# A gate vector computed by four column tiles of the matmul array instead of full-width matmuls, in a tuned attention and feed-forward kernel

## The chip, the cores and the metric

The kernel runs on one core of a Trainium2 chip. The metric is the device time of one execution in microseconds (us); each version is run several times, and what is quoted is the median. Every run used for a verdict is of the fast state. The trace of one execution, taken by the hardware profiler, gives a slightly shorter span than the timed runs: 739.1 us against a median of 741.06 us (740.49 to 744.32, three runs) for the kernel before.

Engines: PE is the matmul engine, PEld its weight loads, DVE the vector engine, ACT the scalar engine, POOL and SP the two that here mostly issue transfers. PSUM is the memory into which PE writes; this kernel uses it as eight banks of 128 partitions by 512 fp32.

## The reference

Two branches on the same input x (2048 rows of 1024, bf16) are mixed by a gate, which is one number per row:

```python
g = sigmoid((x * gate_w).sum(-1, keepdims=True))      # the gate, this case's subject
a = attention(x)        # 32 heads of 32; each row sees 8 rows, 2 apart, itself and backwards
b = (gelu(x @ w_gate) * (x @ w_up)) @ w_down          # 1024 -> 3584 -> 1024
return g * a + (1 - g) * b
```

## The kernel before

The rows are cut into four chunks of 512, and two chunks make a super-chunk: chunks 0 and 1, then 2 and 3. Per super-chunk the phases on PE are: qkv projections, gate logits, the FFN's first two products, then the down projections. Most products use Strassen's scheme with seven block products instead of eight. DVE must first form sums and differences of weight blocks (here called ring forms, because the weights live in a ring of buffers) and of x blocks (x forms, T1 to T4). DVE also does all of the attention's arithmetic except the exponentials.

No order is written by hand. Streams of operations are merged by a scheduler that gives every operation a modelled start, takes the smallest one, and so fixes each engine's order when the kernel is built. Each engine is handed its own list of instructions in that order.

```python
class Weave:                                   # cut
    def _start(self, op):
        ...
        t = self.clk[op.eng]
        for d in deps:
            t = max(t, d.end + (0.04 if d.eng == op.eng else self.LAT + op.lag))
        return t
    def run(self, streams):                    # of all streams' next ops the earliest is emitted
        ...
                if t is not None and (best is None or t + s[0] < best[0]):
                    best = (t + s[0], t, s, op)
...
w.run([(0.0, main()), (0.0, loads()), (0.1, wforms()), (0.1, x_forms()), (0.1, qkv_forms()),
       (0.15, preps()), (0.3, attention()), (0.5, scores())])
```

The gate of a chunk takes eight matmuls, one for each of the eight contraction tiles of 128. The gate weight column is broadcast over all 128 columns of the array, so all 128 output rows of the bank hold the same logits. A transpose in blocks of 32 then puts the logits of 512 rows onto partitions:

```python
def gate(c):
    i, free = bank_take()
    def go():
        for kt in range(KT):                                  # KT = 8
            nc.tensor.matmul(banks[i][:], lhsT=gcol[:, kt:kt + 1].to_broadcast([P, P]), rhs=xT(c, kt),
                             start=(kt == 0), stop=(kt == KT - 1))
    o = pe(KT, go, ...)                                       # modelled cost: 8 matmuls
    yield o
    zt = work.tile([P, SC], F32, tag="u2", bufs=2, name="zt") # buffers shared with u2q below
    e = dve(0.63, lambda: nc.vector.transpose(out=zt[:], in_=banks[i][:]), [o])
    yield e
    bank_give(i, e)
    zc = small.tile([P, SC // 32], F32, tag="zc", bufs=2, name="zc")
    yield dve(0.1, lambda: nc.vector.tensor_scalar(out=zc[:], in0=...zt..., scalar1=ZMAX, scalar2=-ZMAX,
                                                   op0=ALU.min, op1=ALU.max), key=("zc", c))
    ...
def gate_exp(c):                                              # ACT; needs its exp table
    e = act(0.1, lambda: nc.scalar.activation(out=ez[:], in_=zc[:], func=ACT.Exp), [("zc", c)], table="exp", ...)
```

The second super-chunk's gates stand right before its qkv products. The first of these use x as it is (`(0, 0)`, B11); the next need T1 and the first group of ring forms, the next T2 and the second group:

```python
yield from parts[2]                 # down projection of chunk c0
if more:
    yield from halo(c0 + 2)
    yield from gate(c0 + 2)
    yield from gate(c0 + 3)
    yield from qkv_pair(c0 + 2)
...
# qkv_pair, per product, cut:
o = prod(A[t], which, (0, 0), B11, t, True, [fr])             # no form needed
...
o = prod(Dk[t], which, 0, T1, t, True, [fr])                  # ring form 0, one per contraction tile, and T1
    ... ACT copies the bank to m5q
o = prod(Bk[t], which, 1, T2, t, False, [ev["seed", t]])      # ring form 1 and T2
    ... ACT copies the bank to u2q    (tag "u2", bufs=2)
```

Of the kernel before, what the change touches and what calls it, by code (L numbers as in the profile page):

```python
# [9 lines left out]
ALU = mybir.AluOpType  # L10
# [126 lines left out]
def kernel(  # L137
# [61 lines left out]
    banks = [psum.tile([P, SC], F32, name=f"ps{i}") for i in range(8)]  # L199
    xbuf = persist.tile([P, NB, NWIN * AC], BF16)  # L200
    gcol = consts.tile([P, KT], BF16)
    ident = consts.tile([P, P], BF16)
    w = Weave(nc, tc)
    n = NWIN * AC
    V = nc.vector.tensor_tensor
# [1 line left out]
    def xT(c, kt):  # L207
        return xr[:, 2 * (c % 2) + kt // KH, kt % KH, :]
# [18 lines left out]
    def bank_take():  # L227
        best = min(range(len(bank_free)), key=lambda i: -1.0 if bank_free[i][1] is None else bank_free[i][1].end)
        return bank_free.pop(best)

    def bank_give(i, op):
        bank_free.append((i, op))
# [41 lines left out]
        nc.tensor.matmul(banks[7][:], lhsT=warm[:, 0:P], rhs=warm, start=True, stop=True)  # L274
    wj = consts.tile([P, 1], F32)
    nc.scalar.activation(out=wj[:], in_=warm[:, 0:1], func=ACT.Exp)
    make_identity(nc, ident[:])
    nc.vector.memset(kT[0][:, :, 0:HALO], 0.0)
    nc.vector.memset(vT[0][:, :, 0:HALO], 0.0)
    with nc.allow_non_contiguous_dma(reason="gate vector, one element per partition"):  # L280
# [398 lines left out]

    def gate(c):  # L680
        i, free = bank_take()

        def go():
            for kt in range(KT):
                nc.tensor.matmul(banks[i][:], lhsT=gcol[:, kt:kt + 1].to_broadcast([P, P]), rhs=xT(c, kt),  # L685
                                 start=(kt == 0), stop=(kt == KT - 1))
        o = pe(KT, go, ([free] if free else []) + ([("x", c, kt) for kt in range(KT)] if c else []), key=("z", c))
        yield o
        zt = work.tile([P, SC], F32, tag="u2", bufs=2, name="zt")
        e = dve(0.63, lambda: nc.vector.transpose(out=zt[:], in_=banks[i][:]), [o])  # L690
        yield e
        bank_give(i, e)
        zc = small.tile([P, SC // 32], F32, tag="zc", bufs=2, name="zc")
        yield dve(0.1, lambda: nc.vector.tensor_scalar(out=zc[:], in0=zt[:].rearrange("p (b j) -> p b j", j=32)[:, :, 0],
                                                       scalar1=ZMAX, scalar2=-ZMAX, op0=ALU.min, op1=ALU.max),
                  key=("zc", c))
        ez = small.tile([P, SC // 32], F32, tag="ez", bufs=2, name="ez")
        omg = small.tile([P, NST], F32, tag="omg", bufs=3, name="omg")
        gates[c] = (ez, omg, zc)

    def gate_exp(c):
        ez, omg, zc = gates[c]
        e = act(0.1, lambda: nc.scalar.activation(out=ez[:], in_=zc[:], func=ACT.Exp), [("zc", c)], table="exp", lag=1.0,
                key=("ez", c))
        yield e

    def gate_tail(c):
        ez, omg, zc = gates[c]

        def tail():  # L710
            og = small.tile([P, SC // 32], F32, tag="og", name="og")
            nc.vector.tensor_scalar(out=og[:], in0=ez[:], scalar1=1.0, scalar2=1.0, op0=ALU.mult, op1=ALU.add)
            nc.vector.reciprocal(out=og[:], in_=og[:])
            for q in range(4):
                nc.vector.tensor_copy(out=omg[32 * q:32 * (q + 1), :],
                                      in_=og[32 * q:32 * (q + 1), :].rearrange("p (j q) -> p j q", q=4)[:, :, q])
        yield dve(1.2, tail, [("ez", c)], lag=0.6, key=("omg", c))
# [199 lines left out]
            if t + 2 == NT:  # L917
                xb_give(box["ab"], ms[t + 1])

    def ffn(sup, mid):  # L920
        T3, B22, B11, B21 = xr[:, 0], xr[:, 1], xr[:, 2], xr[:, 3]
        T1, T2, T4 = tf[:, 0], tf[:, 1], tf[:, 2]

# [26 lines left out]
        for i in range(FT + 2):  # L950
            if i < FT:
                f = i
                A[f], fr = bank_take()
                o = yield from prod(A[f], "A11", B11, f, True, [fr] + xf)
                Bk[f], fr = bank_take()
                ev[f, "seed"] = act(0.5, lambda f=f: nc.scalar.copy(out=banks[Bk[f]][:], in_=banks[A[f]][:]), [o, fr] if fr else [o])  # L956
                yield ev[f, "seed"]
            while late:
                yield late.pop(0)
            if i >= FT:  # L960
                yield from mid[i - FT]
            if i >= 2:
                f = i - 2
                o = yield from prod(Bk[f], "A22", T4, f, False, [ev[f, "up2"]])
                e = act(0.48, lambda f=f: nc.scalar.copy(out=hs(f, 0), in_=v3(banks[Bk[f]][:])), [o])  # L965
                yield e
                bank_give(Bk[f], e)
                yield dve(tt(2 * SC), lambda f=f: nc.vector.tensor_tensor(  # L968
                    out=hT[:, :, f, :], in0=hT[:, :, f, :], in1=gl[f][:].rearrange("p (j s) -> p j s", s=P), op=ALU.mult),
                    [e, ev[f, "g1"], ev[f, "g2"]], key=("h", sup, f))  # L970
            if i < FT:
                f = i
                Dk[f], fr = bank_take()
                o = yield from prod(Dk[f], 0, T1, f, True, [fr])

                def cp(f=f):
                    m5[f] = work.tile([P, SC], F32, tag="m5", bufs=2, name="m5")
                    nc.scalar.copy(out=m5[f][:], in_=banks[Dk[f]][:])  # L978
                ev[f, "m5"] = act(0.48, cp, [o])
                yield ev[f, "m5"]  # L980
            if 1 <= i < FT + 1:
                f = i - 1
                o = yield from prod(Bk[f], 2, T3, f, False, [ev[f, "u2"]])
                d = [("stored", "o")] if (sup == 0 and f >= 8) else []
                if sup and f >= FT - NT:
                    d = [("qkv", 2 * sup + 1, 0, 0)]
                ev[f, "up2"] = dve(tt(SC, True), lambda f=f: nc.vector.tensor_tensor(  # L987
                    out=hs(f, 1), in0=v3(banks[Bk[f]][:]), in1=v3(m5[f][:]), op=ALU.add), [o, ev[f, "m5"]] + d)
                yield ev[f, "up2"]
            if i < FT:  # L990
                f = i
                o = yield from prod(A[f], "A12", B21, f, False, [ev[f, "seed"]])

                def g1(f=f):
                    gl[f] = work.tile([P, 2 * SC], BF16, tag="gl", bufs=3, name="gl")
                    nc.scalar.activation(out=gl[f][:, SC:2 * SC], in_=banks[A[f]][:], func=ACT.Gelu_apprx_tanh)  # L996
                ev[f, "g1"] = act(0.52, g1, [o], table="gelu")
                yield ev[f, "g1"]
                bank_give(A[f], ev[f, "g1"])
                o = yield from prod(Bk[f], 1, T2, f, False, [ev[f, "seed"]])  # L1000

                def cp2(f=f):
                    u2[f] = work.tile([P, SC], F32, tag="u2", bufs=2, name="u2")
                    nc.scalar.copy(out=u2[f][:], in_=banks[Bk[f]][:])
                ev[f, "u2"] = act(0.48, cp2, [o])
                yield ev[f, "u2"]
                o = yield from prod(Dk[f], 3, B22, f, False, [ev[f, "m5"]])
                e = dve(tt(SC, True), lambda f=f: nc.vector.tensor_tensor(out=u2[f][:], in0=banks[Dk[f]][:],  # L1008
                                                                          in1=u2[f][:], op=ALU.add), [o, ev[f, "u2"]])
                yield e  # L1010
                bank_give(Dk[f], e)
                ev[f, "g2"] = act(0.54, lambda f=f: nc.scalar.activation(out=gl[f][:, 0:SC], in_=u2[f][:],
                                                                         func=ACT.Gelu_apprx_tanh), [e], table="gelu")
                late.append(ev[f, "g2"])
# [139 lines left out]
    def main():  # L1154
        ne = 0
        for j in range(NST):
            for k0 in range(0, KT, KH):
# [2 lines left out]

                def go(pt=pt, j=j, k0=k0):
                    for kk in range(KH):
                        nc.tensor.transpose(out=pt[:, kk, :], in_=hflat(j, k0 + kk, 1), identity=ident[:])  # L1163
                o = Op("PE", 0.3, go, [free] if free else [], tail=0.17)
                yield o
                dst = xr[:, k0 // KH, :, j * P:(j + 1) * P]
# [12 lines left out]
        yield from halo(1)  # L1179
        for which in range(3):  # L1180
            yield from qkv(1, which)
        yield from gate(1)
        for sup in range(NSUP):
            c0 = 2 * sup
            more = sup + 1 < NSUP
            parts = down(c0)
            yield from ffn(sup, parts)
            yield from parts[2]
            if more:
                yield from halo(c0 + 2)  # L1190
                yield from gate(c0 + 2)
                yield from gate(c0 + 3)
                yield from qkv_pair(c0 + 2)
                yield from halo(c0 + 3)
            for part in down(c0 + 1):
                yield from part
            if more:
                yield from q_move(c0 + 3)
# [33 lines left out]
```

## Time and profile before

| | before |
|---|---|
| median of the runs | 741.06 us |
| span in the profile | 739.1 us |
| PE busy | 723.0 us, 98% |
| DVE busy | 630.6 us, 85% |
| four gates on PE, next matmul's start less the gate's | 4 x 1.73 us |
| ACT table loads | 18 |

The page's busy table, one line (busy us, share of the span, number of instructions of each engine):

```profile
...
PE 723.0 (98%) x3298; PEld 358.0 (48%) x3365; DVE 630.6 (85%) x931; ACT 321.6 (44%) x537; POOL 71.2 (10%) x123
...
```

PE is the bound, so time can be won by less work on PE or by less waiting of PE. The view of PE's waits of the kernel before (what waited, for what; us in all, how many times, the longest) names the idle time:

```profile
...
PE ps L927 <- ACT m L978: 3.1, 2, 1.5
PE ps L580 <- DVE ring L547: 1.6, 1, 1.6
...
PE ps L1068 <- DMA ring<-in_A_wo_dram: 1.0, 2, 0.8
...
```

The first line is PE waiting for the scalar engine inside the FFN, at 261 and 549 us, and the second PE waiting for ring forms at 331 us. The third and a similar one of 0.8 us are transfers late between 300 and 319 us.

One gate in the timeline of PE before (start, duration, engine, line, operation, operands, count; matmuls overlap, so the next line's start is the end that matters):

```profile
...
48.16 2.32 PE L464 MATMUL ps<-xr,hT 128*128 128x512 bf16 x10
50.31 1.89 PE L685 MATMUL ps<-xr,gcol 128*128 128x512 bf16 x8
52.04 2.32 PE L464 MATMUL ps<-xr,ring 128*128 128x512 bf16 x10
```

Eight matmuls take 52.04 - 50.31 = 1.73 us, that is 0.216 us each. There is no gap before them: ten matmuls from 48.16 us on end their turn at 50.32 us. The place of the third and fourth gate, and of the ring wait, in the same view (the bracket is idle time before the line and what ended it):

```profile
...
323.50 3.62 PE L685 MATMUL ps<-xr,gcol 128*128 128x512 bf16 x16
326.96 1.89 PE L580 MATMUL ps<-xr,ring 128*128 128x512 bf16 x8
328.68 0.81 PE L580 MATMUL ps<-tf,ring 128*128 128x512 bf16 x3
331.10 2.75 PE L580 MATMUL ps<-tf,ring 128*128 128x512 bf16 x12 [1.60 <-DVE ring L547]
...
```

PE does two gates, eight products from raw weights, three with ring forms, and waits 1.60 us for the fourth form.

The cause of the first ACT wait, in the timeline of ACT before:

```profile
...
255.79 1.28 ACT L703 ACT_TABLE_LOAD   x1
...
257.81 1.28 ACT L1012 ACT_TABLE_LOAD   x1
...
260.22 1.28 ACT L838 ACT_TABLE_LOAD   x1
...
262.05 0.57 ACT L978 COPY m<-ps 128x512 f32<-128x512 f32 x1
...
```

Within 5.7 us ACT loads its table for exp, gelu and exp again (a fourth load follows), 1.28 us each. The copy m at 262.05 us comes late by that, and PE waits 1.53 us for it. The same happens at 549 us.

### The profile page before, as it was taken

To read this page: it belongs to the slowest core of one execution; us is meant where nothing else is said; L and a number is where in the kernel's file an instruction comes from. 1 tells how busy PE (TensorE), PEld (TensorE's weight loads), DVE (VectorE), ACT (ScalarE), POOL (GpSimd) and SP (SyncE) were. 2 spreads that over 40 slices of the span, in tenths; PEclk is the share of its full clock that TensorE was granted. 3 is DMA by queue.
4 is the path that set the end of the run, shared out by engine and by line. 5 is a ranking of instruction groups with operands and counts; after the bars stand their busy time and mean duration, and the time that the engine had idled before them with its cause. 6 is when DMAs were issued, how large, how long until landed. Compare 5 with 4: busy or idle time off the path is not lost.

```text
span 739.1 us, 9823 instructions
## 1 busy us (share of the span) xinstructions
PE 723.0 (98%) x3298; PEld 358.0 (48%) x3365; DVE 630.6 (85%) x931; ACT 321.6 (44%) x537; POOL 71.2 (10%) x123
## 2 busy tenths in 40 slices
PE   8999999999999999989999999999999999999997
PEld 5666644444444444346565444444444444444443
DVE  2789999999999999999999999999999998954300
ACT  2333455558555661125544212765586557210110
POOL 1234522121212000010000001000000000001000
PEclk9999999999999999999999999999999999999999
DMA  9999955555555459990236999745554644899983
GB/s 306 327 329 357 387 173 167 184 171 177 162 180 180 157 147 316 300 327 28 89 112 192 321 308 324 237 135 164 142 159 130 169 139 161 280 307 332 323 288 120
DMA packets 150435, 162.68 MB, mean 220 GB/s; under 512 B 22896, under 2 KB 110960, under 8 KB 150384
## 3 DMA queue, kind: packets, MB, share of 16 engines
q1 hardware_dynamic: 141552, 134.25, 59.6%
q0 software_dynamic: 8544, 27.27, 10.2%
q8 instruction: 26, 0.43, 0.2%
q10 hardware_dynamic: 288, 0.52, 0.2%
q14 instruction: 25, 0.20, 0.1%
HBM read 129.50 MB, written 28.31 MB: 214 GB/s over the span
## 4 chain that ended last, share of the span: by engine, by line
PE 86%; DVE 7%; DMA 2%; ACT 2%; issue 2%; DVEq 0%; ACTq 0%
PE ps L927 44%; PE ps L1068 21%; PE ps L464 11%; PE ps L580 9%; DVE xbuf L879 1%; DMA ring<-dforms 1%; DVE xbuf L887 1%; DVE xbuf L746 1%; DMA ring<-fforms 1%; DVE hT L1036 1%; DVE xbuf L740 0%; DMA hT<-in_A_x_dram 0%; PE ps L685 0%; PE ps L1163 0%; DVE tf L1036 0%
## 5 line engine op out<-in xcount | busy, mean ns | idle before, releaser
L927 PEld LDWEIGHTS <-ring 128*128 128x128 bf16 x1568 | 153.4, 98 | 188.4 <-issue 3.6
L927 PE MATMUL ps<-xr,ring 128*128 128x512 bf16 x878 | 210.4, 379 | 3.9 <-ACT m L978 3.1
L927 PE MATMUL ps<-tf,ring 128*128 128x512 bf16 x659 | 162.6, 379 | 0.8
L1068 PE MATMUL ps<-ring,hT 128*128 128x512 bf16 x693 | 159.7, 379 | 0.9 <-DMA ring<-in_B_w_down_dram 0.2
L1068 PEld LDWEIGHTS <-hT 128*128 128x128 bf16 x708 | 69.2, 98 | 84.0 <-issue 0.7
L740 DVE TENSOR_TENSOR xbuf<-qo,kT 128x2048 bf16<-128x2048 bf16 x64 | 77.5, 1219 | 2.1 <-ACT kT L486 2.1
L879 DVE TENSOR_TENSOR xbuf<-xbuf,vT 128x2048 bf16<-128x2048 bf16 x64 | 77.4, 1219 | 0.2
L746 DVE TENSOR_TENSOR xbuf<-xbuf 128x2048 bf16<-128x2048 bf16 x56 | 68.2, 1219 | 0.2
L580 PEld LDWEIGHTS <-ring 128*128 128x128 bf16 x336 | 43.8, 131 | 30.3 <-DVE ring L547 1.8
L464 PE MATMUL ps<-xr,ring 128*128 128x512 bf16 x250 | 56.1, 383 | 0.4
L956 ACT COPY ps<-ps 128x512 f32<-128x512 f32 x56 | 32.1, 573 | 52.9 <-PE ps L927 52.9
L1095 POOL DMA_DIRECT2D out_dram<-ost x24 | 13.0, 540 | 431.8 <-ACT ost L1103 338.7
L996 ACT ACTIVATE gl<-ps 128x512 bf16<-128x512 f32 x56 | 33.5, 598 | 46.7 <-PE ps L927 46.1
L1068 PE MATMUL ps<-ring,qo 128*128 128x512 bf16 x189 | 49.2, 379 | 2.1 <-DMA ring<-in_A_wo_dram 1.0
L1103 ACT ACTIVATE ost<-ps,omg 128x512 bf16<-128x512 f32 x16 | 11.0, 686 | 91.8 <-PE ps L1068 91.2
L464 PEld LDWEIGHTS <-ring 128*128 128x128 bf16 x256 | 36.9, 144 | 19.4 <-issue 1.3
L580 PE MATMUL ps<-xr,ring 128*128 128x512 bf16 x188 | 43.2, 379 | 0.3
L1008 DVE TENSOR_TENSOR u<-ps,u 128x512 f32<-128x512 f32 x56 | 38.4, 686 | 5.9 <-PE ps L927 2.7
L433 POOL DMA_DIRECT2D fforms<-ring x56 | 30.4, 543 | 124.6 <-DVE ring L425 109.6
L887 DVE TENSOR_TENSOR xbuf<-xbuf 128x1024 bf16<-128x1024 bf16 x64 | 41.8, 687 | 0.5
L968 DVE TENSOR_TENSOR hT<-hT,gl 128x1024 bf16<-128x1024 bf16 x56 | 38.4, 686 | 3.5 <-ACT hT L965 2.6
L987 DVE TENSOR_TENSOR hT<-ps,m 128x512 bf16<-128x512 f32 x56 | 38.5, 687 | 3.0 <-PE ps L927 2.6
(101 smaller groups left out, 736.2 us busy)
## 6 DMA issues: line engine op xcount, KB each, us to landing
ring<-dforms SPq DMA_DIRECT2D x112, 256.0 KB, 4.7
ring<-in_B_w_down_dram SPq DMA_DIRECT2D x84, 256.0 KB, 4.2
ring<-in_B_w_gate_dram SPq DMA_DIRECT2D x56, 256.0 KB, 5.1
fforms<-ring POOLq DMA_DIRECT2D x56, 256.0 KB, 4.3
ring<-fforms SPq DMA_DIRECT2D x56, 256.0 KB, 3.8
ring<-in_B_w_up_dram SPq DMA_DIRECT2D x42, 256.0 KB, 4.0
ring<-in_A_wqkv_dram SPq DMA_DIRECT2D x40, 256.0 KB, 5.7
ring<-oforms SPq DMA_DIRECT2D x32, 256.0 KB, 5.6
```

The source lines that it names most:

```text
L464: nc.tensor.matmul(banks[bk][:], lhsT=lhsT, rhs=xT(c, kt), start=(kt == 0), stop=(kt == KT - 1))
L580: nc.tensor.matmul(banks[bk][:], lhsT=lhsT, rhs=rhs[:, kt, :], start=(start and kt == 0), stop=(kt == KH - 1), skip_group_check=True)
L740: V(out=w3(box[t]), in0=q_b, in1=k_w, op=ALU.mult)
L746: V(out=w3(box[0]), in0=w3(box[0]), in1=w3(box[t]), op=ALU.add)
L879: return dve(tt(n), taking(("p", t), lambda: V(out=w3(box["p", t]), in0=w3(box["ab"]), in1=v_w, op=ALU.mult)), [("qkv", c, 2, t), abo] + ( ...
L887: V(out=s4(t)[:, t % 2], in0=w3(box["p", t])[:, 0:4], in1=w3(box["p", t])[:, 4:8], op=ALU.add)
L927: nc.tensor.matmul(banks[bk][:], lhsT=wv[:, k, fl * P:(fl + 1) * P], rhs=rhs[:, k, :], start=(start and k == 0), stop=(k == KH - 1), skip_ ...
L968: yield dve(tt(2 * SC), lambda f=f: nc.vector.tensor_tensor(out=hT[:, :, f, :], in0=hT[:, :, f, :], in1=gl[f][:].rearrange("p (j s) -> p j ...
L987: ev[f, "up2"] = dve(tt(SC, True), lambda f=f: nc.vector.tensor_tensor(out=hs(f, 1), in0=v3(banks[Bk[f]][:]), in1=v3(m5[f][:]), op=ALU.add ...
L996: nc.scalar.activation(out=gl[f][:, SC:2 * SC], in_=banks[A[f]][:], func=ACT.Gelu_apprx_tanh)
L1008: e = dve(tt(SC, True), lambda f=f: nc.vector.tensor_tensor(out=u2[f][:], in0=banks[Dk[f]][:], in1=u2[f][:], op=ALU.add), [o, ev[f, "u2"]])
L1068: nc.tensor.matmul(banks[bk][:], lhsT=l, rhs=wv[:, i, :], start=(start and k == 0), stop=(q == last and i == 1), skip_group_check=True)
```

## The change

The intent: the eight gate matmuls make 128 equal output rows where one is enough. With four column tiles of 32 columns, four matmuls on different contraction tiles can run side by side, so the gate takes two rounds. The price is that each group of 32 output rows holds only a quarter of the sum. A second step adds the four parts and spreads the sum to all partitions with four small fp32 matmuls against a 0/1 matrix; it is placed later on PE, behind other work. The modelled cost of a gate on PE falls from 8 to 3 matmuls, so that the scheduler knows of it.

```diff
     def gate(c):
...
-            for kt in range(KT):
-                nc.tensor.matmul(banks[i][:], lhsT=gcol[:, kt:kt + 1].to_broadcast([P, P]), rhs=xT(c, kt),
-                                 start=(kt == 0), stop=(kt == KT - 1))
-        o = pe(KT, go, ...)
+            for r in range(KT // 4):
+                for q in range(4):
+                    kt = 4 * r + q
+                    nc.tensor.matmul(banks[i][32 * q:32 * (q + 1), :], lhsT=gcol[:, kt:kt + 1].to_broadcast([P, 32]),
+                                     rhs=xT(c, kt), start=(r == 0), stop=(r == KT // 4 - 1),
+                                     tile_position=(0, 32 * q), skip_group_check=True)
+        o = pe(KT // 4 + 1, go, ...)
...
+        zq = small.tile([P, SC // 32], F32, tag="zq", bufs=2, name="zq")
+        e = dve(0.1, lambda: nc.vector.tensor_copy(out=zq[:], in_=...zt...), [e], key=("zq", c))
+    def gate_sum(c):
+        i, free = bank_take()
+            for q in range(4):
+                nc.tensor.matmul(banks[i][32 * q:32 * (q + 1), 0:SC // 32], lhsT=qsum[:], rhs=zq[:], start=True, stop=True,
+                                 tile_position=(0, 32 * q), skip_group_check=True)
+        o = pe(1, go, [("zq", c)] + ...)
+        e = dve(0.1, ... tensor_scalar(out=zc[:], in0=banks[i][:, 0:SC // 32], ZMAX, -ZMAX, min, max) ..., key=("zc", c))
...
             if more:
                 yield from halo(c0 + 2)
                 yield from gate(c0 + 2)
                 yield from gate(c0 + 3)
                 yield from qkv_pair(c0 + 2)
+                yield from gate_sum(c0 + 2)
+                yield from gate_sum(c0 + 3)
```

(The sums of chunks 0 and 1 stand behind the first qkv product of chunk 1 and in the second step of the FFN; the 0/1 matrix is made by POOL at the start; the identity matrix for the first transposes moves into a buffer that is free then, to make room.)

More of the change, by code (lines that the diff above doesn't have):

```diff
@@ L201 @@
     gcol = consts.tile([P, KT], BF16)
-    ident = consts.tile([P, P], BF16)
+    ident = hT[:, NST + 1, 0, :]
     w = Weave(nc, tc)
@@ L276 @@
     nc.scalar.activation(out=wj[:], in_=warm[:, 0:1], func=ACT.Exp)
-    make_identity(nc, ident[:])
+    make_identity(nc, ident)
+    qsum = consts.tile([P, 32], F32)
+    nc.gpsimd.memset(qsum[:], 0.0)
+    for d in range(-P + 32, 1, 32):
+        nc.gpsimd.affine_select(out=qsum[:], in_=qsum[:], compare_op=ALU.not_equal, fill=1.0, base=d,
+                                pattern=[[-1, 32]], channel_multiplier=1)
     nc.vector.memset(kT[0][:, :, 0:HALO], 0.0)
@@ L681, in gate @@
         i, free = bank_take()
+        dx = [("x", c, kt) for kt in range(KT)] if c else []
         def go():
-            for kt in range(KT):
-                nc.tensor.matmul(banks[i][:], lhsT=gcol[:, kt:kt + 1].to_broadcast([P, P]), rhs=xT(c, kt),
-                                 start=(kt == 0), stop=(kt == KT - 1))
-        o = pe(KT, go, ([free] if free else []) + ([("x", c, kt) for kt in range(KT)] if c else []), key=("z", c))
+            for r in range(KT // 4):
[4 more added lines that the diff above has]
+                                     tile_position=(0, 32 * q), skip_group_check=True)
+        o = pe(KT // 4 + 1, go, ([free] if free else []) + dx, key=("z", c))
         yield o
@@ L692, in gate, with go @@
         bank_give(i, e)
+        zq = small.tile([P, SC // 32], F32, tag="zq", bufs=2, name="zq")
+        e = dve(0.1, lambda: nc.vector.tensor_copy(out=zq[:], in_=zt[:].rearrange("p (b j) -> p b j", j=32)[:, :, 0]), [e],
+                key=("zq", c))
+        yield e
         zc = small.tile([P, SC // 32], F32, tag="zc", bufs=2, name="zc")
-        yield dve(0.1, lambda: nc.vector.tensor_scalar(out=zc[:], in0=zt[:].rearrange("p (b j) -> p b j", j=32)[:, :, 0],
-                                                       scalar1=ZMAX, scalar2=-ZMAX, op0=ALU.min, op1=ALU.max),
-                  key=("zc", c))
         ez = small.tile([P, SC // 32], F32, tag="ez", bufs=2, name="ez")
         omg = small.tile([P, NST], F32, tag="omg", bufs=3, name="omg")
-        gates[c] = (ez, omg, zc)
+        gates[c] = (ez, omg, zc, zq)
+    def gate_sum(c):
+        i, free = bank_take()
+        zc, zq = gates[c][2:]
+        def go():
+            for q in range(4):
+                nc.tensor.matmul(banks[i][32 * q:32 * (q + 1), 0:SC // 32], lhsT=qsum[:], rhs=zq[:], start=True, stop=True,
+                                 tile_position=(0, 32 * q), skip_group_check=True)
+        o = pe(1, go, [("zq", c)] + ([free] if free else []))
+        yield o
+        e = dve(0.1, lambda: nc.vector.tensor_scalar(out=zc[:], in0=banks[i][:, 0:SC // 32], scalar1=ZMAX, scalar2=-ZMAX,
+                                                     op0=ALU.min, op1=ALU.max), [o], key=("zc", c))
+        yield e
+        bank_give(i, e)
     def gate_exp(c):
-        ez, omg, zc = gates[c]
+        ez, zc = gates[c][0], gates[c][2]
         e = act(0.1, lambda: nc.scalar.activation(out=ez[:], in_=zc[:], func=ACT.Exp), [("zc", c)], table="exp", lag=1.0,
@@ L707, in gate_tail @@
     def gate_tail(c):
-        ez, omg, zc = gates[c]
+        ez, omg = gates[c][:2]
         def tail():
@@ L918, in att_half, with ffn @@
                 xb_give(box["ab"], ms[t + 1])
-    def ffn(sup, mid):
+    def ffn(sup, mid, early=()):
         T3, B22, B11, B21 = xr[:, 0], xr[:, 1], xr[:, 2], xr[:, 3]
@@ L959, in ffn @@
                 yield late.pop(0)
+            if i == 1:
+                for g in early:
+                    yield from g
             if i >= FT:
@@ L1162, in go @@
                     for kk in range(KH):
-                        nc.tensor.transpose(out=pt[:, kk, :], in_=hflat(j, k0 + kk, 1), identity=ident[:])
+                        nc.tensor.transpose(out=pt[:, kk, :], in_=hflat(j, k0 + kk, 1), identity=ident)
                 o = Op("PE", 0.3, go, [free] if free else [], tail=0.17)
@@ L1181, in main @@
             yield from qkv(1, which)
+            if which == 0:
+                yield from gate_sum(0)
         yield from gate(1)
@@ L1186, in main @@
             parts = down(c0)
-            yield from ffn(sup, parts)
+            yield from ffn(sup, parts, [gate_sum(1)] if sup == 0 else [])
             yield from parts[2]
```

## The prediction

> **What bounds the kernel now.** TensorE. The busy table gives PE 723.0 of a 739.1 us span (98%), DVE 630.6 (85%), ACT 321.6 (44%). Timeline: eight 512-column matmuls take 1.73 us. PE's waits: 3.1 us in two waits on ACT (copies of m) inside the FFN, at 261 and 549 us; 1.6 us on DVE (Strassen forms of the qkv weights, ring) at 331 us; about 2 us on DMA between 300 and 319 us. The chain of waits leaves PE for ACT at 255 to 262 us, then runs on DVE from 269 to 331 us: DVE decides when the second half's qkv products start.
>
> **What the change removes.** Four gates of eight 128-column matmuls: 4 x 1.73 = 6.9 us of PE, all on PE's path.
>
> **What it adds on PE.**
> - Per gate, two rounds of four column tiles. The Trainium skill, "TensorE: Matmul & The Clock Gate", Part 3, measures 2.38x for three column tiles at N=512, so the tiles overlap; ideal is 2 x 0.216 = 0.43 us. "TensorEngine Tiling (Array Packing)", Tiling Modes, says that switching mode drains the array; this trace has a 0.379 us record for a matmul spaced 0.216, so about 0.16 us of pipe per drain (estimate). I expect 0.8 us per gate (0.6 to 1.2), 3.7 us saved in all.
> - Four gate sums, each four fp32 matmuls of 16 columns with their drains: 0.7 us each (0.3 to 1.2, an estimate from nothing in this trace but the drain), 2.8 us in all.
>
> Net on PE: about -1 us.
>
> **What it moves.** A scheduler reorders everything by modelled times. The two programs' orders show:
> - ACT table loads fall from 18 to 11. Before, the exps of chunks 1 and 2 fall inside the FFN and bring exp-gelu-exp-gelu, four loads of 1.28 us; each group makes a 1.53 us PE wait. After, chunk 1's exps come where no gelu follows, and chunk 2's two share one load. I expect both waits to go: -3.0 us of PE idle.
> - On DVE, most of the softmax steps of chunk 1's second half (about 3 us) move behind the qkv forms, so these are ready about 3 us earlier. But PE, with shorter gates, arrives earlier too: the two zt transposes and x forms still stand before the last first-product forms, so a wait on ring of about 1 to 2.5 us stays. This stretch is set by DVE, so of all PE gains before 331 us only about 3 us survive there.
> - Eight small DVE operations (zc takes 0.18 us) and five POOL ones cost nothing.
>
> **Sum.** About 3 us by the start of the paired qkv, +1.5 for the ACT wait at 549, -1.4 for the last two gate sums: 741.06 - 3.3 = 737.7 us. Range 733.5 to 741.5. Over 2% (14.8 us) exceeds the idle time named.
>
> **What would show it.** Right: gate matmuls of one round starting together, a gate spanning under 1.2 us; the waits on m gone; 11 table loads; the first ring-form product starting about 3 us before 331 us. Wrong: gate tiles in series (0.2 us apart); gate sums over 1.5 us; new waits of PE on DVE (ring, forms of S) or DMA (ring).
>
> **What would make it wrong.** The static order: an ACT exp waiting in order for DVE inside the FFN, holding PE's copies; DMA waits at 300 to 319 us that grow because PE arrives earlier; slow fp32 matmuls.

## The result

| | before | changed |
|---|---|---|
| median of the fast runs | 740.77 us (739.85 to 744.32, 4 runs) | 740.39 us (739.99 to 740.91, 4 runs) |
| ratio | | 0.9988, 95% interval 0.9964 to 1.0012 |
| span in the profile | 739.1 us | 738.2 us |
| mean granted clock of PE in the profile | 1.000 | 0.995 |
| a gate on PE, from its first start to the next matmul's | 1.73 us | 0.55 us |
| the same with the gap before it | 1.73 us | 0.64 us |
| a gate sum on PE, without and with the gap before it | none | 0.19 and 0.28 us, two together 0.25 and 0.34 us |
| ACT table loads | 18 | 11 |
| PE waits for ACT | 3.1 us | none |
| PE waits for ring forms | 1.6 us | 7.7 us |

A ratio here and below is worked out from all fast runs of a kernel and of the kernel before in the same set, so it is not quite the ratio of the two medians.

The time lies in the predicted range, but 2.7 us above the predicted value. That range was 8 us wide and held the kernel before's own 741.06 us, so lying in it says little. Nearly all of what was hoped for happened, and more, and then it was lost. The gate, in the timeline of PE of the changed kernel:

```profile
...
48.26 1.67 PE L469 MATMUL ps<-xr,hT 128*128 128x512 bf16 x7
49.87 0.61 PE L693 MATMUL ps<-xr,gcol 128*32 128x512 bf16 x8
50.41 3.89 PE L469 MATMUL ps<-xr,ring 128*128 128x512 bf16 x17
```

50.41 - 49.87 = 0.54 us for the same eight contraction tiles. Two rounds of one matmul time are 0.43 us, so about 0.11 us is left over. But a gap also stands before the gate: seven matmuls from 48.26 us on end their turn at 49.77 us, and the gate starts 0.10 us later (0.09 us from the unrounded starts). The kernel before has no such gap. So a gate costs PE 0.64 us, about 0.2 us more than two matmul times. The trace's records show the overlap itself: the four matmuls of the first round start within 0.01 us, and those of the second 0.226 us after them. The gate sums, in the view of that line's instructions (how many; ns least, median, most; first and last start):

```profile
...
L717 PEld LDWEIGHTS ps<-zq,qsum x32: 106/109/113, 64.4 to 401.7; 128*32 128x32 f32 x32
L717 PE MATMUL ps<-zq,qsum x32: 182/183/204, 64.4 to 401.7; 128*32 128x16 f32 x32
...
```

The programme has 16 such matmuls and the trace 32 records of each kind, so each fp32 matmul appears as two. On PE's time line the four of one gate take 98.37 - 98.18 = 0.19 us, and 0.09 us more with the gap before them. With the gaps counted, two single gates of 0.64 us and a pair of 1.07 us replace 4 x 1.73 us, which saves 4.6 us; the sums cost 2 x 0.28 + 0.34 = 0.9 us. Net, the change gives PE 3.7 us.

The busy line and the waits of PE of the changed kernel, in that order:

```profile
...
PE 723.9 (98%) x3397; PEld 355.7 (48%) x3397; DVE 631.1 (85%) x935; ACT 312.7 (42%) x530; POOL 72.0 (10%) x128
...
```

```profile
...
PE ps L585 <- DVE ring L552: 7.7, 3, 4.2
...
PE ps L1096 <- DMA ring<-in_A_wo_dram: 0.6, 2, 0.4
```

The wait for ACT is gone, the waits for transfers have fallen, and the wait for ring forms has grown from 1.6 to 7.7 us. Its three parts in PE's timeline:

```profile
...
318.03 1.05 PE L693 MATMUL ps<-xr,gcol 128*32 128x512 bf16 x16
319.01 1.95 PE L585 MATMUL ps<-xr,ring 128*128 128x512 bf16 x8
322.81 0.41 PE L585 MATMUL ps<-tf,ring 128*128 128x512 bf16 x1 [1.86 <-DVE ring L552]
324.89 0.41 PE L585 MATMUL ps<-tf,ring 128*128 128x512 bf16 x1 [1.67 <-DVE ring L552]
329.45 4.88 PE L585 MATMUL ps<-tf,ring 128*128 128x512 bf16 x14 [4.16 <-DVE ring L552]
...
```

The gates start 5.5 us earlier than before and end 8.0 us earlier. But the products with ring forms run freely only from 329.45 us, 1.65 us earlier than before (331.10). What stood in the way is seen in DVE's timeline of the changed kernel; DVE has no idle time here:

```profile
...
321.24 1.18 DVE L449 TENSOR_TENSOR tf<-xr 128x2048 bf16<-128x2048 bf16 x1
322.35 0.41 DVE L552 TENSOR_TENSOR ring<-ring 128x512 bf16<-128x512 bf16 x1
322.68 1.22 DVE L451 TENSOR_TENSOR tf<-xr,tf 128x2048 bf16<-128x2048 bf16 x1
323.81 0.69 DVE L835 TENSOR_TENSOR xbuf<-xbuf 128x1024 bf16<-128x1024 bf16 x1
324.41 0.42 DVE L552 TENSOR_TENSOR ring<-ring 128x512 bf16<-128x512 bf16 x1
324.75 0.69 DVE L838 TENSOR_TENSOR xbuf<-xbuf 128x512 f32<-128x512 bf16 x1
325.35 0.71 DVE L699 STREAM_TRANSPOSE zt<-ps 128x512 f32<-128x512 f32 x1
325.98 1.18 DVE L453 TENSOR_TENSOR xr<-xr 128x2048 bf16<-128x2048 bf16 x1
327.09 0.17 DVE L703 COPY zq<-zt 128x16 f32<-128x16 f32 x1
327.17 0.71 DVE L699 STREAM_TRANSPOSE zt<-ps 128x512 f32<-128x512 f32 x1
327.80 1.18 DVE L454 TENSOR_TENSOR tf<-xr,tf 128x2048 bf16<-128x2048 bf16 x1
328.90 0.17 DVE L703 COPY zq<-zt 128x16 f32<-128x16 f32 x1
328.98 4.78 DVE L552 TENSOR_TENSOR ring<-ring 128x512 bf16<-128x512 bf16 x14
...
```

PE needs L449 (T1) and four of L552 (ring form 0) for its next product. DVE does T1 at 321.24 us and two of the forms by 324.8 us. Then come a fold of the softmax, a transpose of the gates, an x form that is needed later, a copy, another transpose, another x form and another copy, and the third ring form starts only at 328.98 us. The order was fixed when the kernel was built.

While PE stands still, its clock is taken away. The view by stretches of the changed kernel (busy us and instructions of each engine; PEclk is the mean granted clock):

```profile
...
core 0: us, PE busy (x) PEld busy (x) DVE busy (x) ACT busy (x) POOL busy (x), PEclk, DMA share, GB/s
320.00:325.00 5.00, 1.47 (x7) 0.59 (x5) 5.00 (x7) 1.14 (x2) 0.04 (x1) 1.00 0.89 336
325.00:330.00 5.00, 0.84 (x3) 0.33 (x3) 5.00 (x11) 0.00 (x0) 0.00 (x0) 0.61 0.01 3
330.00:335.00 5.00, 5.00 (x18) 2.23 (x17) 4.90 (x16) 2.34 (x4) 0.00 (x0) 0.71 0.00 0
...
```

In 325 to 330 us the mean is 0.61 and in the next five 0.71. If the clock is either full or half, that is (1 - 0.61) x 5 / 0.5 = 3.9 us and 2.9 us at half, 6.8 us together; the trace's own clock record says 6.83 us. About half of it falls on real matmuls after 329.45 us. The Trainium skill, "TensorE: Matmul & The Clock Gate", Part 1, says that an idle window of about 3.4 us halves the clock. This trace agrees in the main: the half clock began at 326.07 us, after 5 us in which PE had done but two matmuls, so the window before it was not wholly idle, and it lasted two times 3.41 us.

Where time was won and lost, from the starts of PE's phases in the two timelines (us from the span's start):

| PE starts | before | changed | difference so far |
|---|---|---|---|
| first gate | 50.31 | 49.87 | -0.44 (start of the run) |
| first FFN | 95.21 | 92.89 | -2.32 (two gates, one sum) |
| first down projection | 263.53 | 259.82 | -3.71 (first ACT wait gone) |
| third gate | 323.50 | 318.03 | -5.47 (less waiting for transfers) |
| paired qkv products | 326.96 | 319.01 | -7.95 (two gates) |
| after the last ring wait | 331.10 | 329.45 | -1.65 (ring waits) |
| second down projection | 401.03 | 401.86 | +0.83 (half clock, sums) |
| second FFN | 455.42 | 456.26 | +0.84 |
| third down projection | 623.73 | 622.89 | -0.84 (second ACT wait gone) |

Within the paired qkv phase everything won before it is lost. Two things must be told apart by experiment: what the gates are worth and what the new order is worth, and whether the wait is the fault of DVE's order or of DVE's amount of work.

### The profile page after: what moved, and what is told of

It is laid out like the page before. It is cut to its first block, busy times and chain, and to the rows that moved or that the text cites. A ratio compares the mean times of both kernels' runs of the same rounds, so it can differ in the third digit from the quotient of the medians.

```text
span 738.2 us, 9955 instructions
## 1 busy us (share of the span) xinstructions
PE 723.9 (98%) x3397; PEld 355.7 (48%) x3397; DVE 631.1 (85%) x935; ACT 312.7 (42%) x530; POOL 72.0 (10%) x128
## 4 chain that ended last, share of the span: by engine, by line
PE 95%; DMA 3%; DVE 1%; issue 0%; ACT 0%; DVEq 0%
PE ps L952 46%; PE ps L1096 28%; PE ps L469 11%; PE ps L585 10%; DMA ring<-in_A_wo_dram 1%; DMA ring<-oforms 1%; DMA ring<-in_A_wqkv_dram 1%; DMA hT<-in_A_x_dram 0%; PE ps L1191 0%; DVE zt L699 0%; DVE tf L451 0%; DVE tf L449 0%; PE ps L693 0%; DVE ring L552 0%; ACT ost L1131 0%
## 5 line engine op out<-in xcount | busy, mean ns | idle before, releaser
L952 PE MATMUL ps<-tf,ring 128*128 128x512 bf16 x672 | 164.0, 379 | 0.0
L585 PE MATMUL ps<-tf,ring 128*128 128x512 bf16 x144 | 35.1, 394 | 7.7 <-DVE ring L552 7.7
```

Of the source, the lines that this page charges most:

```text
L585: nc.tensor.matmul(banks[bk][:], lhsT=lhsT, rhs=rhs[:, kt, :], start=(start and kt == 0), stop=(kt == KH - 1), skip_group_check=True)
L952: nc.tensor.matmul(banks[bk][:], lhsT=wv[:, k, fl * P:(fl + 1) * P], rhs=rhs[:, k, :], start=(start and k == 0), stop=(k == KH - 1), skip_ ...
```

## The experiments

Twelve kernels ran, in three sets of four, each set on one chip with its own runs of the kernel before (medians 740.54, 739.88 and 740.74 us). All gave a correct result. In the names, a_ is made from the changed kernel, b_ from the kernel before, and w_ from the changed one with wide gates.

The theory at the start: what PE won ahead of 331 us is lost to the place of the ring forms in DVE's fixed order, and the wait also costs clock. The rivals: DVE is late as a whole, whatever its order; or the clock costs nothing; or the gate is dearer than it looks.

### a_again: the changed kernel once more

> The changed kernel once more, unaltered, as the yardstick of this set on the same chip. Both theories: within 0.2% of 740.4 us, ratio to before 0.998 to 1.000; PE waits for DVE (ring) about 7.7 us around 321 to 329 us, and the granted clock drops to half for about 6.8 us there (mean 0.995).

Measured: 740.25 us (5 runs), ratio 0.9993 (0.9978 to 1.0008); ring wait 7.5 us; mean clock 0.993. The wait and the loss of clock are not a chance of one profile. In this one the half clock lasted 10.24 us, three times 3.41. The kernel before loses clock too, though not in the run whose trace was kept: in this set five of its eleven runs have a mean of 0.997 or 0.998 and a median of 741.16 us, the six at 1.000 one of 739.76 us. So a good part of the spread of its runs goes with the clock.

### a_warm: matmuls without use keep the clock up

```diff
                 for kt in range(KH):
+                    if which == 0 and form == 0 and t == 0 and keep:
+                        for _ in range((8, 7, 18, 0)[kt]):
+                            nc.tensor.matmul(banks[keep['bank']][:], lhsT=xr[:, 2, 0, 0:P], rhs=B11[:, 0, :],
+                                             start=True, stop=True, skip_group_check=True)
```

(They write to a bank that is free and is given back. Their modelled cost is zero, so nothing else moves.)

> The changed kernel with 33 matmuls whose result is thrown away, put where PE waits for the ring forms (8, 7 and 18 of them, 1.7, 1.5 and 3.9 us), no other order touched. Theory (the wait of 7.7 us also costs clock: the half clock runs on for about 3.4 us of real matmuls, 1.7 us lost): granted clock 1.000, time 1.7 us below the changed kernel, about 738.7 us. Rival (the dip of the clock falls into idle time and costs nothing): same time as the changed kernel within 0.5 us.

Measured: 738.55 us (5 runs), ratio 0.9970 (0.9955 to 0.9985), clock 1.000. That is 1.7 us below a_again of the same set. Of the ring waits this is left:

```profile
...
PE ps L591 <- DVE ring L552: 0.3, 1, 0.3
...
```

PE is no less held up, it is only busy with nothing: it gets to the third ring form at 329.58 us, in a_again at 329.64 us. From there to the last two gate sums it takes 70.60 us against 72.24 us, 1.64 us less. So the half clock costs 1.7 us by itself, and the rival that it falls into idle time is out.

### a_hoist and b_hoist: the ring forms moved forward on DVE

The scheduler's model is left alone; only the emission of some DVE operations is put off until others have been emitted:

```diff
+    def until(op):          # between T1 and the last of the 16 ring forms of the first qkv product
+        ...
+        if op.key in (T2, T3, T4):  return last form of group 0, 1, 2
+        return last form of group 3          # everything else that stands between
```

> The changed kernel with the order on DVE altered in one place: the 16 ring forms of the first qkv product and the four x forms stand right after each other; two softmax folds and the gates' transposes and copies come after them. PE and ACT orders unchanged. Theory (what PE gained before 331 us, about 8 us at the end of the gates, was lost to the place of the ring forms in DVE's fixed order): the ring wait falls from 7.7 us to 1 to 3 us, the clock stays at 1.000, time 5 to 7 us below the changed kernel, 733.5 to 735.5 us. Rival 1 (DVE as a whole is too late, whatever its order, or the weights land too late): the wait only moves to later forms or to DMA, gain under 2 us. Rival 2 (the gate itself is dearer than it looks): no gain.

> The same alteration of DVE's order in the kernel before. Theory: there PE reaches the ring forms about 8 us later and waits only 1.6 us, so the gain is at most 1.6 us: 738.5 to 740.5 us. Then the change is worth, at a place where DVE does not bind, the difference of the two altered kernels: 4.5 to 6 us. Rival (the forms' place costs both kernels alike): both altered kernels gain the same.

Measured: a_hoist 740.49 us (6 runs), ratio 0.9999 (0.9981 to 1.0017), no gain; b_hoist 742.56 us, ratio 1.0025 (1.0009 to 1.0040), slower. Both miss what was expected. The waits of PE in a_hoist:

```profile
...
PE ps L598 <- ACT u2q L642: 5.0, 1, 5.0
PE ps L598 <- DVE ring L565: 2.0, 2, 1.8
...
```

The ring wait did fall to 2.0 us. But a wait of 5.0 us for ACT's copy u2q is new. It has a plain cause in the code: u2q and the gates' zt share two buffers (tag u2), and I had put the transposes' readers behind all sixteen forms, to 333.9 us. b_hoist has the same wait, 3.5 us. The experiment was badly made, and its times say nothing yet on the theory.

### a_hoist2 and b_hoist2: the same, with the gates' transposes after the second group

```diff
+        if ".gate." in op.fn.__qualname__:
+            return ("wq", 2, 0, 1, 3)            # last ring form of group 1
         return ("wq", 2, 0, 3, 3)
```

> As a_hoist, but the gates' two transposes zt and their copies stand after the second group of ring forms instead of behind all sixteen. In a_hoist the ring wait fell to 2.0 us as expected, but PE then waited 5.0 us for ACT's copy u2q, whose buffer (tag u2, two of them) is the one the gates' zt uses, and which was held until the late copies zq. Theory (ring forms' place was the loss; the u2q wait was an artefact of my order): ring wait 2 to 3 us, no wait on u2q over 0.5 us, clock 1.000, time 733.5 to 736 us, ratio to before 0.990 to 0.994. Rival (DVE has too much work before this point, so any order only moves the wait): a wait of 4 us or more at another product of the first qkv group, and a time within 1 us of the changed kernel.

> The same order in the kernel before. In b_hoist the ring wait went but a u2q wait of 3.5 us came. Theory: both waits gone, 738.5 to 740 us, at most 1.6 us below before, so that the change is worth 4 to 6 us where DVE's order does not eat it. Rival: the kernel before gains as much as the changed one.

Measured: a_hoist2 737.23 us (5 runs), ratio 0.9960 (0.9947 to 0.9973), clock 1.000; b_hoist2 739.57 us, ratio 0.9987 (0.9976 to 0.9999). The changed kernel, whose own order has 0.9988 and 0.9993 in the other sets, wins 2.1 to 2.4 us by order alone, the kernel before 1 us or less. But the gain is half of what was expected. The waits of PE in a_hoist2:

```profile
...
PE ps L598 <- DVE qo L659: 2.4, 1, 2.4
PE ps L598 <- DVE ring L565: 2.0, 3, 1.7
...
```

The ring wait is 2.0 us as expected, and 2.4 us are lost again at the first result that DVE has to fetch from a bank (qo), which now stands behind the softmax steps that were moved back. So the ring forms' place was a loss, and this order makes another one. b_hoist2 shows the second alone: its ring wait is gone, and 1.5 us of waiting for the same result have taken its place. Whether DVE simply has too much to do here, or only this order is bad, a_hoist3 below decides.

### b_cost3: the kernel before, in an order made for short gates

```diff
-        o = pe(KT, go, ...)
+        o = pe(3, go, ...)            # modelled cost only; still eight full matmuls
```

> The kernel before with nothing but the scheduler's modelled cost of a gate altered, 3 matmuls' time instead of 8 (the changed kernel's figure); the gate itself is the old one. The recorded order alone moves: 16 table loads instead of 18, the four-load group in the first FFN gone, the one in the second FFN kept. Theory (the two ACT waits are the order's work, not the gate's): the ACT wait at about 261 us gone, the one at about 549 us still 1.5 us; since PE then reaches the ring forms 1.5 us earlier and these are not earlier, the ring wait grows from 1.6 to about 3 us; time 740 to 741.5 us. Rival (the gate's speed removes the ACT waits): both ACT waits as before.

Measured: 742.80 us (6 runs), ratio 1.0038 (1.0026 to 1.0051): 2.8 us slower, more than expected. The waits of PE:

```profile
...
PE ps L580 <- DVE ring L547: 5.5, 2, 4.5
...
PE ps L927 <- ACT m L978: 1.3, 1, 1.3
...
```

One of the two ACT waits is gone and the other is there (1.3 us), with the old gates. So the first belongs to the order, as expected; for the second see a_wide. The ring wait is 5.5 us, also with the old gates, and the clock is halved for 6.83 us. So this order is harmful with the old gates. It is not the changed kernel's order, which a_wide tests.

### a_qouter: does it matter in which order the column tiles are fed?

```diff
-            for r in range(KT // 4):
-                for q in range(4):
+            for q in range(4):
+                for r in range(KT // 4):
```

> The changed kernel with the eight gate matmuls in the other order: both contraction tiles of one column tile, then the next column tile. The same matmuls, the same sums. If column tiles overlap only while neighbours in the instruction order are on different tiles: the gate spans about 1.1 us (five times 0.216) instead of 0.55. If they run freely whatever the order: still 0.55 us. If nothing overlapped (ruled out by 0.55): 1.7 us.

Measured (one look, 741.98 us, state unknown): the gate in PE's timeline

```profile
...
49.50 0.62 PE L693 MATMUL ps<-xr,gcol 128*32 128x512 bf16 x8
50.06 4.11 PE L469 MATMUL ps<-xr,ring 128*128 128x512 bf16 x18
```

takes 50.06 - 49.50 = 0.56 us. The order is of no account: two matmuls in a row on one column tile do not hold up the next tile. The records say more: four matmuls start within 0.02 us at 49.50 us and the other four from 49.73 us on. The program has both of one tile next to each other, and two on one tile need a turn of 0.216 us each, so the second one of the first tile must have started after the first one of the last tile, out of the program's order (worked out from the starts; a record does not name its tile). The profile has a 2.0 us wait on ACT at 104 us that the profiles of the same order (changed, a_again) do not have.

### a_wide: the changed kernel's order with the old gates

```diff
-    nc.tensor.matmul(banks[i][32 * q:32 * (q + 1), :], lhsT=gcol[:, kt:kt + 1].to_broadcast([P, 32]), rhs=xT(c, kt),
-                     start=(r == 0), stop=(r == KT // 4 - 1), tile_position=(0, 32 * q), skip_group_check=True)
+    nc.tensor.matmul(banks[i][:], lhsT=gcol[:, kt:kt + 1].to_broadcast([P, P]), rhs=xT(c, kt),
+                     start=(kt == 0), stop=(kt == KT - 1))
-        ... compare_op=ALU.not_equal, fill=1.0, ...
+        ... compare_op=ALU.not_equal, fill=0.25, ...
```

> The changed kernel with its own recorded order on every engine, but the gate's eight matmuls 128 columns wide and one after the other, as before (the 0/1 matrix then holds 0.25, since each row already has the whole sum). PE is given back 4 x 1.18 = 4.7 us of work. Theory (in this order DVE decides when the ring-form products start, so what the gates saved ahead of 331 us is worth nothing): PE resumes at about 329.5 us as before, the ring wait falls from 7.7 to about 3 us, the clock dip is gone or shorter; time 738 to 740.5 us, not slower than the changed kernel. Rival (the gates' saving is in the result, and the order costs the rest): 744 to 745.5 us.

Measured: 742.32 us (5 runs), ratio 1.0021 (1.0008 to 1.0035), outside what the theory expected and below what the rival did. The ring wait is 5.1 us, not 3, and the half clock lasted 6.83 us as in the changed kernel. PE waits for ACT nowhere here, with the old gates: so both ACT waits of the kernel before belong to the order. Against the changed kernel (0.9993 and 0.9988 in the other sets) it is 0.3% slower, 2.1 to 2.5 us. So the gates' saving is worth about half of its 4.6 us here (4.7 in the expectation, which left out the gap before a gate). PE's timeline shows which half:

```profile
...
324.75 1.89 PE L585 MATMUL ps<-xr,ring 128*128 128x512 bf16 x8
...
327.77 0.41 PE L585 MATMUL ps<-tf,ring 128*128 128x512 bf16 x1 [0.92 <-DVE ring L552]
332.33 5.94 PE L585 MATMUL ps<-tf,ring 128*128 128x512 bf16 x14 [4.16 <-DVE ring L552]
...
```

PE comes to the paired qkv products at 324.75 us, 5.7 us later than in the changed kernel (319.01), and leaves the ring wait at 332.33, only 2.9 us later (329.45). T1 on DVE also starts 2.9 us later, at 324.12 instead of 321.24 us. That is where the theory was too simple: DVE does not run on its own ahead of this point. In the FFN it takes part in every step of PE, so that the two gates before the FFN bring DVE forward as well (first FFN product at 92.89 against 95.78 us, again 2.9 us). Of these 2.9 us, 0.7 was there before the first gate (49.87 against 50.54 us), a difference between two executions; 2.2 us are the two gates'. Their saving lasts. The two gates that stand right before the paired qkv products bring only PE forward, not DVE, and theirs is lost in the ring wait.

### a_hoist3, w_hoist3, b_hoist3: the better order for the changed kernel, for the old gate in it, and for the kernel before

```diff
     def until(op):
+        if ".att_half." in op.fn.__qualname__ and op.eng in ("DVE", "ACT") and T1 emitted and last evacuation of the
+                first qkv group not yet emitted:
+            return that evacuation
```

> As a_hoist2, and the softmax steps of the attention half in hand (two folds, three maxima, the subtraction) stand on DVE behind the four evacuations of the first qkv group; a_hoist2 left a PE wait of 2.4 us for the first of those. Theory: that wait goes, ring wait about 2 us, clock 1.000, time 734 to 736 us. Rival (DVE short of time whatever the order): a new wait of over 1.5 us within the next qkv group, time 737 us.

> a_hoist3 with the wide, serial gates of a_wide: the worth of the column tiles alone where the order no longer eats it. Theory: PE has 4.7 us more work, of which the ring wait of about 2 us takes up a part: 2.5 to 4.7 us slower than a_hoist3, 737 to 739.5 us. Rival (gates worth nothing anywhere): same as a_hoist3.

> The kernel before with the same order as a_hoist3 at this place. Its two ACT waits (3.1 us) and its wide gates stay, the DVE waits in the first qkv group go: 737.5 to 739.5 us, so 3 to 5 us slower than a_hoist3. Rival: it gains as much as the changed one and ends within 1 us of a_hoist3.

| | median | ratio to before | 95% interval |
|---|---|---|---|
| a_hoist3 | 735.93 us | 0.9930 | 0.9917 to 0.9942 |
| w_hoist3 | 737.76 us | 0.9957 | 0.9944 to 0.9969 |
| b_hoist3 | 739.63 us | 0.9976 | 0.9962 to 0.9990 |

a_hoist3 beats the kernel before by 4.8 us and, by the ratios of the three sets, the changed kernel by 4.3 to 4.7 us, with three moves in DVE's and ACT's order. What PE still waits for in its paired qkv products:

```profile
...
PE ps L598 <- DVE ring L565: 1.2, 3, 0.9
...
PE ps L598 <- ACT ps L620: 1.1, 1, 1.1
...
PE ps L598 <- ACT u2q L642: 0.4, 1, 0.4
...
```

2.7 us are left of 7.7, the clock stays at full (1.000), and the new wait is 1.1 us, below the rival's 1.5. The 2.4 us wait for qo is gone too, so it was the order and not DVE's amount of work; of the 7.7 us of ring wait, order explains at least 5.0. w_hoist3 is 1.8 us slower than a_hoist3, less than expected: in its profile the ring wait is 0.2 us instead of 1.2, and the phase from the first paired qkv product to its end is 2.0 us shorter (323.72 to 399.68 against 319.23 to 397.23). Here too DVE takes back most of what the last two gates save. b_hoist3 gains only 1.1 us by the medians (1.8 by the ratio), and it is 3.7 us slower than a_hoist3: with this place repaired in both, that is what the whole change is worth, against 0.4 us as it was made. Not all of it is the column tiles' work. b_hoist3 keeps its 3.1 us of ACT waits, which belong to the order, and w_hoist3, with wide gates and the changed kernel's order, is already 1.9 us faster than b_hoist3; the tiles add 1.8 us. The kernel before, with its own gates and no sums, was not built in an order free of the ACT waits, so it was not tried at its best.

## Why the prediction was right or wrong

**PE is the bound, by 98%.** Right as an average, and right as the reason why the total moved little. In the stretch that decided the result, though, it was DVE.

**The gate's own cost.** Right, at the low end of the range. Expected 0.8 us per gate (0.6 to 1.2), measured 0.64 us with the gap before it (0.55 us without). The Trainium skill, "TensorE: Matmul & The Clock Gate", Part 3, gives 2.38 times for three column tiles; here four give 1.73 / 0.64 = 2.7 times, with the changes of mode counted in. "TensorEngine Tiling (Array Packing)", Tiling Modes, says that changing the mode drains the array. The trace has 0.09 us of gap before a gate and 0.10 us after it; my estimate of 0.16 us for each of two drains was too high. That the gaps are this drain fits, but no run isolates it.

**The gate sums.** Expected 0.7 us each (0.3 to 1.2), measured 0.28 us with the gap before it, and 0.34 us for two together. Net on PE the change gave 3.7 us where about 1 us was forecast.

**The ACT waits.** Right: table loads 18 to 11, both waits gone, 3.1 us. b_cost3 for the first wait and a_wide for both show that this came from the order and not from the gate.

**The step that failed** is this one of the prediction: the ring forms "are ready about 3 us earlier", and "a wait on ring of about 1 to 2.5 us stays". The mechanism was named, down to the transposes and x forms that stand before the last forms; two terms of its sum were mis-sized. The forms were ready 1.65 us earlier, not 3, and PE arrived 8.0 us earlier, so the wait was 7.7 us. The forms gained less because DVE itself ran behind. Counted by the views by stretches, DVE had done 269.9 us of work by 300 us against 272.0 before. At the end of the attention half in hand (the last write of qo) it was 3.0 us late, 305.1 against 302.1 us, and the softmax steps that had been moved behind the forms only just made up for that. Part of this is a wait of 1.6 us for a weight transfer at 84 us that was not there before; the rest is spread out and was not traced further.

**What was not foreseen at all** is the clock: an idle stretch of that length halves it, and this took 1.7 us (a_warm against a_again). It was not in the list of what could go wrong, though the skill's page has it.

**"Of all PE gains before 331 us only about 3 us survive there."** The idea was right, and 1.65 us survived. Then 2.5 us were lost up to the second down projection, 0.8 us more than had survived: 1.7 us to the clock, 0.3 us to two sums, and about 0.4 us that was not traced. a_wide shows which gains survive: those of the two gates before the FFN, about 2.2 us, because DVE moves with PE there; not those of the two gates right before the wait.

**The sum.** Forecast -3.3 us, measured -0.4 us. That the time still fell into the range is partly luck, since errors of opposite sign cancelled: PE's work fell by 2.7 us more than forecast and its waits for transfers by 1.4 us, which was not forecast; the ring wait was over 5 us longer than forecast, and the clock's 1.7 us were not foreseen. In terms of the experiments: the order, with the gate sums and their small DVE operations, costs 1.6 us (a_wide against before), and the column tiles in that order bring back about 2.1 us.

**"DMA waits that grow because PE arrives earlier"** did not come; they fell from about 2 to 0.6 us.

One thing stays open. Why the scheduler puts the last ring forms behind the gates' transposes was only argued. Its model gives each transfer a time, and if the model's transfers are later than the chip's, it will place DVE work for them too late. The trace does show that the data were there: SP issued the last x transpose at 308.64 us and the weights from 309.89 us on, and in a_hoist the first eight ring forms ran from 321.98 us on without any idle time of DVE.

## What to carry to other kernels

Before shortening work on the busiest engine, look at what it does next and who supplies that. In this kernel, work saved far ahead of a hand-over brought the supplier forward too and lasted; work saved right before it turned into a wait, and several microseconds of waiting on PE also cost clock. When a scheduler fixes the orders, a change of one modelled cost is a change of the whole order: measure the new order with the old work and the new work separately, and repair the order at the place that waits before judging the change.

## What the Trainium skill lacked or had wrong

- "TensorEngine Tiling (Array Packing)" gives no figure for the drain at a change of mode. Here a gate of two rounds on four column tiles, between full-width matmuls, took 0.54 to 0.56 us to the next matmul's start, after a gap of 0.09 us: 0.64 to 0.65 us in all, 0.21 to 0.22 us above two matmul times of 0.216 us.
- "TensorE: Matmul & The Clock Gate", Part 3, has three column tiles at 2.38 times. Four, with 128 rows of contraction and 512 columns, gave 2.7 times with both gaps counted (1.73 to 0.64 us), whichever of two orders of the tiles was used (a_qouter 0.65 us).
- "FP8 and Floating Point Precision", TensorE Precision Notes, speaks of four passes for true fp32 and of no time. In the trace each small fp32 matmul (128 rows, 32 columns, 16 moving columns) is two weight loads and two matmuls, and four of them take 0.19 us of PE's time, 0.28 us with the gap before them. How many passes a record holds is not visible.
- The same clock page says that idle windows halve the clock. It was borne out: half clock for 3.41, 6.83 and 10.24 us in the middle of different runs, always a multiple of 3.41 us. But the window need not be wholly idle: in a_again the half clock began at 323.03 us, after a wait of 2.1 us and some 1.1 us of matmuls before it, while in a_hoist2 a wait of 2.4 us left the clock full. The page's Terms price it at the throttled time times the share of clock withheld, which would be 6.83 x 0.5 = 3.4 us. Here it was 1.7 us, because half of the throttled time fell on a PE that waited, and 33 matmuls without use put in the gap avoided it.
